# Decay attention and a mixer on one core: k of one pair turned by VectorE, the state's scan ahead of a masked copy, two loads a place later

## The chip, the cores and the metric

One core of a Trainium2 chip runs the whole computation in one launch. TensorE (PE) multiplies and transposes, VectorE (DVE) and ScalarE (ACT) work on its results in PSUM, GpSimd (POOL) works on data in SBUF, and SyncE (SP) issues nearly all loads and stores, which 16 DMA engines carry out. The metric is the device time of the launch in microseconds (us). A profile records one execution in which every instruction has a start and a duration. The page of the profile and the views quoted below are drawn from it.

## The reference

An attention with decay, in blocks of 64 rows, then a mixer over tokens and over channels. All arrays of the attention are float32; the mixer's four weights are float64.

```python
# q, k, v: (4, 8, 768, 64); lam: (8,)
for b in range(nb):                                    # blocks of 64 rows
    intra = einsum('bhic,bhjc->bhij', qb, kb) * Dmask  # lam ** (i - j), lower triangle
    intra = einsum('bhij,bhjd->bhid', intra, vb)
    inter = einsum('bhid,bhde->bhie', qb * lam_pow, kv_state)
    out[:, :, sl] = intra + inter
    kv_state = lam_block * kv_state + einsum('bhsd,bhse->bhde', kb * rev_pow, vb)
x = out.transpose(0, 2, 1, 3).reshape(4, 768, 512)

xt = x.transpose(0, 2, 1)
h = np.maximum(xt @ w_tok1, 0.0) @ w_tok2              # 768 -> 256 -> 768, over tokens
u = x + h.transpose(0, 2, 1)
h2 = np.maximum(u @ w_ch1, 0.0) @ w_ch2                # 512 -> 1536 -> 512, over channels
return u + h2
```

## The kernel before

**The attention stage.** The work is cut into 16 pairs of heads (4 batches, 4 pairs each), with rows in six blocks of 128. A loop written out by hand runs over `i` from -2 to 15; the instructions stand on each engine's queue in just this order, and each queue runs in order. Iteration `i` computes the scores of pair `i + 1`, the outputs of pair `i`, and prepares pair `i + 2`:

- `scores(i + 1)`, for each half `g` of the rows: PE multiplies k by q into two PSUM banks (`sc`, L304), and DVE multiplies them by the decay mask into SBUF (`a`, L312, "masked copy").
- `outputs(i, 0)`: PE adds scores times v (L328) and scaled q times state (L338); ACT copies the result to `uT` (L345).
- `state(i + 1)`: PE makes the products of k and v per block (`kv`, L270), DVE runs a scan over the blocks (`sv`, L278), and later, as `place()`, POOL copies it to `stb` (L291).
- `outputs(i, 1)`, the same for the second half.
- k and q of pair `i + 2` are turned so that the head dimension lies on partitions. For early pairs PE does it with transposes, three blocks to a PSUM bank, and ACT copies the bank out: `turn_q_rows` (L241, L242) for pairs below `NQ` = 5, `turn_k` (L220, L225) for pairs below `NKD` = 8. For later pairs DVE does it in one instruction (`turn_q` L230, `turn_kr` L234) from data that is loaded a second time, in another order, in pieces of 32 columns (`load_dims`, L115, four loads of 96 KB with rows of 128 bytes).
- `turn_back(i, g)`: PE turns the outputs back (`xp`, L360), ACT writes the high part `xhi` (L368), DVE the low part `xlo` (L369).
- `scale_k(i + 2)`: k times a decay, L250 on ACT and L252 on POOL; from pair `NKD` on both heads on ACT. `scale_q` (L257) is on POOL.

PSUM banks are taken in turn: three with the tag `sh`, and one `xT` that is lent out after the outputs. `kv`, `xp`, `kt`, `qt` and the groups of the mixer all share them, so that the next group on PE can wait for DVE's scan or for ACT's copy of an older one.

**The mixer's groups** fill the rest: from iteration 4 on, `take` says how many groups of the token mixer (`token_hidden` with `ph` L456, `hh` L460, `hl` L461; `token_out` with `pu` L493 and the addition L498) an iteration runs.

**The weights** come as float64 words and are made float32 by `narrow`: one step on ACT (L387) and four on DVE (L388, L391, L394, L397), then `split` into a high and a low part (L379 on ACT, L380 on POOL). These steps are put into a list `waiting`, and calls of `later(n)` between the other steps of the loop take a few off it. w1 comes in three parts, converted after iterations 0, 1 and 2; w2 comes in one load of 1536 KB, issued in iteration 3 and converted from iteration 5 on.

**The loads** of the loop all stand on SP's queue, in the order of the program. At the end of iteration `i`:

```python
if i == -1:
    load_w1(0)
if 0 <= i + 3 < NI and i >= -1:
    load_v(i + 3)
if i == -1:
    load_w1(1)
if i + 4 < NI:
    load_kq(i + 4)
if i == -1:
    load_w1(2)
if i == 3:
    load_w2()
```

`load_kq` issues k, q and, for pairs from `NKD` on, `kr`. The buffers of k, q and `kr` are two deep, those of v three.

After the loop the token mixer ends and the channel mixer runs to the end of the span; the change doesn't touch it.

Of the kernel before, what the change touches and what calls it, by code (L numbers as in the profile page):

```python
# [9 lines left out]
F32 = mybir.dt.float32  # L10
# [12 lines left out]
def kernel(  # L23
# [23 lines left out]
    nc = tc.nc  # L47
# [4 lines left out]
    P = 128  # L52
# [43 lines left out]
    ap = att.enter_context(tc.tile_pool(name="att", bufs=1))  # L96

    pairs = [(b, p) for b in range(B) for p in range(NP)]
# [3 lines left out]


    NQ = 5
    NKD = 8
    loaded = {}

    krs = {}
# [23 lines left out]
    def load_kq(i):  # L132
# [11 lines left out]
        else:  # L144
            load_dims(qn, q, b, p)
        if i >= NKD:
            kr = kp.tile([P, S], F32, tag="kr", bufs=2, name=f"kr{i}")
# [16 lines left out]
    mask = ap.tile([P, H, P], F32, name="mask")  # L164
# [35 lines left out]
    while n < P:  # L200
        nc.vector.tensor_mul(
            out=lamp[:, :, n : 2 * n], in0=lamp[:, :, 0:n], in1=lamp[:, :, n - 1 : n].broadcast_to([P, NP, n])
        )
        n *= 2
    for p in range(NP):
        nc.gpsimd.tensor_copy(
            out=keep[:, p, :, 1:], in_=lamp[:, p, P - 1 : P, None].broadcast_to([P, D, NC - 2])
# [4 lines left out]
    kTs, qTs, qss, kds, weights_of = {}, {}, {}, {}, {}  # L212
# [50 lines left out]
    def state(i):  # L263

        b, p = pairs[i]
        kv = bank("sh", f"kv{i}", D * (NC - 1))
        to = kv.rearrange("p (e c) -> p c e", c=NC - 1)
        for c in range(NC - 1):
            for h in range(2):
                nc.tensor.matmul(  # L270
                    out=to[h * D : (h + 1) * D, c, :],
                    lhsT=kds[i][:, h, c, :],
                    rhs=vns[i][:, h, c, :],
                    start=(c == 0),
                    stop=(c == NC - 2),
                )
        sv = ap.tile([P, D * (NC - 1)], F32, tag="sv", bufs=1, name=f"sv{i}")
        nc.vector.tensor_tensor_scan(  # L278
            out=sv,
            data0=keep[:, p].rearrange("p e c -> p (e c)"),  # L280
            data1=kv,
            initial=0.0,
            op0=ALU.mult,
            op1=ALU.add,
        )
        st = stb[i % 2]

        def place():
            for h in range(2):
                r = slice(h * D, (h + 1) * D)  # L290
                nc.gpsimd.tensor_copy(out=st[r, :, h, :], in_=sv[r].rearrange("p (e c) -> p c e", c=NC - 1))  # L291

        return place

    def scores(i):
        b, p = pairs[i]
        for g in range(2):
            pair = two_banks(f"sc{i}{g}", 3 * P)
            sc = [pair[:, h] for h in range(2)]
            for c in range(3):  # L300
                cs = slice((3 * g + c) * P, (3 * g + c + 1) * P)
                for h in range(2):
                    r = slice(h * D, (h + 1) * D)
                    nc.tensor.matmul(  # L304
                        out=sc[h][:, c * P : (c + 1) * P],
                        lhsT=kTs[i][r, cs],
                        rhs=qTs[i][r, cs],
                        start=True,
                        stop=True,
                    )  # L310
            a = ap.tile([P, 2, 3, P], F32, tag="a", bufs=4, name=f"a{i}{g}")
            nc.vector.tensor_mul(  # L312
                out=a,
                in0=pair.rearrange("p h (c i) -> p h c i", i=P),
                in1=mask[:, 2 * p : 2 * p + 2, None, :].broadcast_to([P, 2, 3, P]),
            )
            for h in range(2):
                weights_of[i, g, h] = a[:, h]

    def outputs(i, g):  # L320
        b, p = pairs[i]
# [80 lines left out]
    def words(b):  # L402
        return uT[b].rearrange("p t s -> p (t s)").bitcast(U32)

    def load_w1(i):
        cs = slice(2 * i, 2 * i + 2)
        nc.sync.dma_start(
            out=words(3).rearrange("p (c f) -> p c f", c=NC)[:, cs],
            in_=w_tok1.bitcast(U32).rearrange("(c s) f -> s c f", s=P)[:, cs],
        )  # L410
# [225 lines left out]
        groups.extend(hidden[b] + outs[b])  # L636
    take = {4: 2, 5: 2, 6: 2, 7: 5, 8: 4, 9: 4, 10: 5, 11: 2, 12: 2, 13: 4, 14: 3, 15: 1}
    early = {4: 2}
    LATE = 7
    idle = [lambda: None]  # L640
    held = [groups[n] for n in (36, 37, 33, 34, 35)]
# [5 lines left out]

    for i in range(-2, NI):
        if 0 <= i + 1 < NI:
            scores(i + 1)  # L650
            scale_q(i + 1)
        if i >= 0:
            outputs(i, 0)
        place = state(i + 1) if 0 <= i + 1 < NI else None
        work = [groups.popleft() for _ in range(take.get(i, 0))]
        if i == NI - 1:
            work.pop(0)()
        if i >= 0:
            outputs(i, 1)
            spare.append("xT")  # L660
        if i + 2 < NI and i != LATE:
            turn_q(i + 2)
            if i + 2 >= NKD:
                turn_kr(i + 2)
        if i + 2 < NI:
            if 0 < i + 2 < NP:
                masks(i + 2)
            turns = [(turn_k, 0), (turn_k, 1)] if i + 2 < NKD else []
            if i + 2 < NQ:
                turns += [(turn_q_rows, 0), (turn_q_rows, 1)]  # L670
            if i == -2:
                turns.sort(key=lambda x: x[1])
            for f, g in turns:
                f(i + 2, g)
        if place:
            place()
        later(0 if i == NI - 1 else 1 if work else 2)
        n = early.get(i, len(work) // 4)
        cuts = [0, n, max(n, (3 * len(work) + 1) // 4 if len(work) > 2 else len(work) // 2), len(work)]
        for n in range(3):  # L680
            for f in work[cuts[n] : cuts[n + 1]]:
                f()
                later(2 if len(work) < 3 else 1)
            if n < 2 and i >= 0:
                turn_back(i, n)
                later(1 if work else 2 + n)
            if n == 0 and i + 2 < NI:
                scale_k(i + 2)
        if i == -1:
            load_w1(0)  # L690
        if 0 <= i + 3 < NI and i >= -1:
            load_v(i + 3)
        if i == -1:
            load_w1(1)
        if i + 4 < NI:
            load_kq(i + 4)
        if i == -1:
            load_w1(2)
        if i == 3:
            load_w2()  # L700
        if 0 <= i < 3:
            convert_w1(i)
        if i == 5:
            weights[0] = group_tiles(0, False)
            w3 = words(3)
            load_piece(0, 0, w3[:, 2048:3072])
        if i == 4:
            convert_w2(0)
            convert_w2(1)
        if i == 5:  # L710
            convert_w2(2)
        if i == 6:
            waiting.append(lambda: load_piece(0, 1, w3[:, 1024:2048]))
            steps = narrow_piece(w3[:, 2048:3072], w3[:, 0:512], w3[:, 512:1024])
            turns = [lambda: turn_q(LATE + 2), lambda: turn_kr(LATE + 2)]
            waiting.extend(steps[:1] + 2 * idle + turns[:1] + idle + turns[1:] + idle + steps[1:2] + idle + steps[2:])
        if i == 7:
            steps = narrow_piece(w3[:, 1024:2048], w3[:, 512:1024], w3[:, 2048:2560])
            waiting.extend(steps[:1] + 2 * idle + steps[1:])
            waiting.append(lambda: load_piece(0, 2, w3[:, 2048:3072]))  # L720
        if i == 8:
            waiting.extend(split_c1(weights[0], w3[:, 0:512], w3[:, 512:1024], nc.gpsimd))
        if i == 9:
            waiting.append(lambda: load_piece(0, 3, w3[:, 1024:2048]))
            waiting.extend(narrow_piece(w3[:, 2048:3072], w3[:, 0:512], w3[:, 512:1024]))
            waiting.append(split_c2(weights[0], 2, w3[:, 0:512]))
        if i == 10:
            homes[0] = {"B11": (up, None, 1), "B21": (up, None, 1), "T2": (kp, "kn", 2), "T1": (kp, "qn", 2)}
            homes[0] |= {"B22": (kp, "kr", 2), "T3": (kp, "kT", 2), "T4": (kp, "qT", 2)}
            first = build(0, 0, on_vector=("T1", "T2", "T3", "T4", "B22"))  # L730
            waiting.extend([first["B11"], first["B21"]])
            waiting.extend(narrow_piece(w3[:, 1024:2048], w3[:, 2048:2560], w3[:, 2560:3072]))
            waiting.append(split_c2(weights[0], 3, w3[:, 2048:2560]))
        if i == 11:
            later(99)
        if i == 13:
            for xs in (("t1",), ("t2", "T1.h"), ("T2.h", "T1.l"), ("T2.l", "t3", "t4"), ("T3.h", "T4.h"), ("T3.l", "T4.l")):
                waiting.append(lambda xs=xs: [first[x]() for x in xs])
# [583 lines left out]
    for jj, x in [(jj, x) for jj in (1, 0) for x in range(4)]:  # L1322
        c, es, _, copy, queue = last_pieces[x]
# [30 lines left out]
```

## Time and profile before

| | |
|---|---|
| median of 3 runs | 554.91 us (554.79 to 555.17) |
| the profiled execution's own time | 554.8 us |
| its span, first to last instruction | 553.0 us |
| mean granted TensorE clock | 1.000 |
| busy: PE, DVE, ACT, POOL | 542.2, 437.2, 247.4, 281.6 us |
| attention stage | up to about 165 us |

The page gives busy time per engine; a busy PE isn't one at its peak, since ends of matmuls are modelled. The table of stages gives busy times for stretches of the span, the granted clock, the mean busy share of the 16 DMA engines and what they moved. In the lines of a timeline, the first two numbers are start and duration in us, and the bracket at the end, where there is one, is the time that the engine sat idle before it and who released it. The chain that ended last is followed back from the last instruction; its lines are start, duration, engine and line.

### The profile page before, as it was taken

The numbers are of one execution on the slowest core, as the hardware profiler recorded it, in microseconds if no ns is written. First come the engines' busy times: TensorE is split into PE (matmuls) and PEld (weight loads), VectorE is DVE, ScalarE is ACT, GpSimd is POOL, SyncE is SP. The second block draws the span as 40 slices with busy tenths as digits, with TensorE's granted clock in tenths as the row PEclk, the third lists the DMA queues.
The fourth block names the chain that finished last, engine by engine and source line by source line (L and its number), as shares of the span: only waits on it lengthen the run. The fifth ranks groups of instructions, "written<-read, shape, count | busy, mean of one in ns | idle before, by whom it ended". The sixth has DMA issues, their size and how long they took to land.

```text
span 553.0 us, 10803 instructions
## 1 busy us (share of the span) xinstructions
PE 542.2 (98%) x4180; PEld 528.3 (96%) x4180; DVE 437.2 (79%) x657; ACT 247.4 (45%) x499; POOL 281.6 (51%) x256
## 2 busy tenths in 40 slices
PE   6999999999999999999999999999999999999997
PEld 4888998999999999999999999999999999999996
DVE  4787889697786989887878878788777877788894
ACT  3464452335262554343444443443454555445431
POOL 5667453657214564444435444354475656568550
PEclk9999999999999999999999999999999999999999
DMA  9998999998203433361725300024767131220176
GB/s 182 252 208 170 232 186 176 195 196 145 50 2 98 181 114 124 101 223 39 248 78 181 142 1 1 0 30 59 149 137 199 58 116 57 86 105 2 22 155 129
DMA packets 175683, 66.77 MB, mean 121 GB/s; under 512 B 163600, under 2 KB 165904, under 8 KB 175632
## 3 DMA queue, kind: packets, MB, share of 16 engines
q1 hardware_dynamic: 170400, 64.90, 49.0%
q10 hardware_dynamic: 5232, 1.18, 1.0%
q8 instruction: 33, 0.54, 0.4%
q14 instruction: 18, 0.15, 0.1%
HBM read 49.29 MB, written 16.78 MB: 119 GB/s over the span
## 4 chain that ended last, share of the span: by engine, by line
PE 89%; DVE 4%; DMA 3%; ACT 1%; issue 1%; SPq 1%; ACTq 0%; DVEq 0%
PE po L1033 22%; PE pa L807 13%; PE pc L807 9%; PE pb L807 7%; PE pa L1007 7%; PE pc L1007 5%; PE ph L456 5%; PE sc L304 4%; PE pu L493 3%; PE xT L328 3%; PE pd L807 3%; DMA qn<-in_q_dram 3%; PE xT L338 2%; PE pu L476 2%; PE xp L360 1%; PE kv L270 1%
## 5 line engine op out<-in xcount | busy, mean ns | idle before, releaser
L1046 DVE TENSOR_TENSOR uT<-po,uT 128x768 f32<-128x768 f32 x57 | 54.2, 952 | 17.1 <-PE po L1033 16.8
L822 ACT ACTIVATE c<-c 128x384 f32<-128x384 f32 x42 | 22.1, 526 | 59.2 <-DVE c L867 33.5
L291 POOL COPY stb<-sv 64x320 f32<-64x320 f32 x32 | 26.7, 833 | 41.4 <-DVE sv L278 40.5
L1013 DVE TENSOR_TENSOR uT<-pa,uT 128x768 f32<-128x768 f32 x36 | 34.3, 953 | 10.3 <-PE pa L1007 9.6
L328 PE MATMUL xT<-a,vn 128*64 128x128 f32 x384 | 35.7, 277 | 0.0
L824 POOL TENSOR_TENSOR h22l<-c,h22h 128x384 fp32r<-128x384 f32 x14 | 14.4, 1032 | 41.5 <-ACT h22h L823 41.5
L345 ACT COPY uT<-xT 128x384 f32<-128x384 f32 x32 | 15.3, 479 | 44.2 <-PE xT L338 44.1
L1013 DVE TENSOR_TENSOR uT<-pc,uT 128x768 f32<-128x768 f32 x27 | 25.8, 954 | 11.2 <-PE pc L1007 11.2
L312 DVE TENSOR_TENSOR a<-sc,mask 128x768 f32<-128x768 f32 x32 | 29.1, 948 | 4.6 <-PE sc L304 4.5
L338 PE MATMUL xT<-qs,stb 128*64 128x128 f32 x320 | 31.3, 273 | 0.0
L380 POOL TENSOR_TENSOR c1l<-cs,c1h 128x512 fp32r<-128x512 f32 x15 | 19.3, 1298 | 23.1 <-ACT c1h L379 23.1
L456 PE MATMUL ph<-xhi,w1h 128*128 128x256 f32 x96 | 28.2, 293 | 0.7 <-DVE sv L278 0.4
L1033 PE MATMUL po<-h12h,c 128*128 128x384 f32 x112 | 28.7, 337 | 0.0
L1033 PE MATMUL po<-h11h,c 128*128 128x384 f32 x112 | 28.6, 336 | 0.0
L1033 PE MATMUL po<-h22h,c 128*128 128x384 f32 x112 | 28.6, 336 | 0.0
L1033 PE MATMUL po<-h21h,c 128*128 128x384 f32 x112 | 28.6, 336 | 0.0
L304 PE MATMUL sc<-qT,kT 64*128 64x128 f32 x384 | 27.1, 290 | 0.3 <-ACT qT L242 0.2
L304 PEld LDWEIGHTS sc<-qT,kT 64*128 64x128 f32 x384 | 23.9, 196 | 3.5 <-issue 1.7
L456 PE MATMUL ph<-xhi,w1l 128*128 128x256 f32 x96 | 27.1, 282 | 0.0
L456 PE MATMUL ph<-xlo,w1h 128*128 128x256 f32 x96 | 27.1, 282 | 0.0
L369 DVE TENSOR_TENSOR xlo<-xp,xhi 128x384 fp32r<-128x384 f32 x32 | 17.7, 553 | 11.0 <-ACT xhi L368 10.8
L257 POOL TENSOR_TENSOR qs<-qT,lamp 128x640 f32<-128x640 f32 x16 | 25.5, 1592 | 0.3
(397 smaller groups left out, 1944.0 us busy)
## 6 DMA issues: line engine op xcount, KB each, us to landing
raw<-in_moe_w_ch_dram SPq DMA_DIRECT2D x20, 512.0 KB, 3.7
vn<-in_v_dram SPq DMA_DIRECT2D x16, 384.0 KB, 5.3
kn<-in_k_dram SPq DMA_DIRECT2D x30, 192.0 KB, 5.4
out_dram<-y SPq DMA_DIRECT2D x104, 48.0 KB, 1.9
qn<-in_q_dram SPq DMA_DIRECT2D x44, 96.0 KB, 4.0
kr<-in_k_dram SPq DMA_DIRECT2D x32, 96.0 KB, 2.7
dc1h<-c1h SPq DMA_DIRECT2D x4, 768.0 KB, 5.3
dc1l<-c1l SPq DMA_DIRECT2D x4, 768.0 KB, 6.7
```

The lines of the kernel that those rows point to most:

```text
L257: nc.gpsimd.tensor_mul(out=qss[i], in0=qTs[i][:, P:].rearrange("p (c i) -> p c i", i=P), in1=lamp[:, p, None, :].broadcast_to([P, NC - 1, P]),
L291: nc.gpsimd.tensor_copy(out=st[r, :, h, :], in_=sv[r].rearrange("p (e c) -> p c e", c=NC - 1))
L304: nc.tensor.matmul(out=sc[h][:, c * P : (c + 1) * P], lhsT=kTs[i][r, cs], rhs=qTs[i][r, cs], start=True, stop=True,)
L312: nc.vector.tensor_mul(out=a, in0=pair.rearrange("p h (c i) -> p h c i", i=P), in1=mask[:, 2 * p : 2 * p + 2, None, :].broadcast_to([P, 2, ...
L328: nc.tensor.matmul(out=xT[h * D : (h + 1) * D, cs], lhsT=vns[i][:, h, c, :], rhs=weights_of[i, g, h][:, cg, :], start=(cg == 0), stop=False,)
L338: nc.tensor.matmul(out=xT[h * D : (h + 1) * D, cs], lhsT=st[:, c - 1, h, :], rhs=qss[i][:, c - 1, :], start=False, stop=(cg == 2),)
L456: nc.tensor.matmul(out=ph, lhsT=w[:, c, fs], rhs=x[:, c], start=(i == 0), stop=(i == 3 * NC - 1))
L807: nc.tensor.matmul(out=to, lhsT=w[:, t], rhs=x[:, t], start=(start and i == 0), stop=(i == 5), skip_group_check=not start,)
L1007: nc.tensor.matmul(out=pair[x][:, t], lhsT=w[:, t], rhs=h, start=(start and i == 0), stop=(i == 2), skip_group_check=not start,)
L1013: nc.vector.tensor_add(out=ub, in0=pair[x], in1=ub)
L1033: nc.tensor.matmul(out=to, lhsT=w[:, jj, t * P : (t + 1) * P], rhs=h, start=(i == 0), stop=(i == 3 * JG - 1))
L1046: nc.vector.tensor_add(out=ub, in0=po, in1=ub)
```

## The change

Three edits:

1. `NKD` goes from 8 to 7: k of the eighth pair (`i` = 7) is turned by DVE in `turn_kr(7)` in iteration 5 and not by PE in `turn_k(7, 0)` and `turn_k(7, 1)`. `load_kq(7)`, in iteration 3, loads `kr` of pair 7 as well, and `scale_k(7)` has both heads on ACT.
2. In pairs 3, 4, 5, 7 and 8 (`SCAN_FIRST`), the second masked copy (`g` = 1) is issued after `state`, and so behind the scan on DVE's queue.
3. Part 1 of w1 is loaded after k and q of pair 3, and part 2 after k and q of pair 4, an iteration later.

```diff
-    NKD = 8
+    NKD = 7
...
+    def mask_scores(i, g, pair):
+        p = pairs[i][1]
+        a = ap.tile([P, 2, 3, P], F32, tag="a", bufs=4, name=f"a{i}{g}")
+        nc.vector.tensor_mul(
+            out=a,
+            in0=pair.rearrange("p h (c i) -> p h c i", i=P),
+            in1=mask[:, 2 * p : 2 * p + 2, None, :].broadcast_to([P, 2, 3, P]),
+        )
+        for h in range(2):
+            weights_of[i, g, h] = a[:, h]
+
     def scores(i):
-        b, p = pairs[i]
         for g in range(2):
             pair = two_banks(f"sc{i}{g}", 3 * P)
...
-            a = ap.tile([P, 2, 3, P], F32, tag="a", bufs=4, name=f"a{i}{g}")
-            nc.vector.tensor_mul(
-                out=a,
-                in0=pair.rearrange("p h (c i) -> p h c i", i=P),
-                in1=mask[:, 2 * p : 2 * p + 2, None, :].broadcast_to([P, 2, 3, P]),
-            )
-            for h in range(2):
-                weights_of[i, g, h] = a[:, h]
+            if g == 0 or i not in SCAN_FIRST:
+                mask_scores(i, g, pair)
+        return pair
...
+    SCAN_FIRST = (3, 4, 5, 7, 8)
...
         if 0 <= i + 1 < NI:
-            scores(i + 1)
+            pair = scores(i + 1)
             scale_q(i + 1)
         if i >= 0:
             outputs(i, 0)
         place = state(i + 1) if 0 <= i + 1 < NI else None
+        if i + 1 in SCAN_FIRST:
+            mask_scores(i + 1, 1, pair)
...
         if 0 <= i + 3 < NI and i >= -1:
             load_v(i + 3)
-        if i == -1:
-            load_w1(1)
         if i + 4 < NI:
             load_kq(i + 4)
-        if i == -1:
-            load_w1(2)
+        if -1 <= i < 1:
+            load_w1(i + 2)
         if i == 3:
             load_w2()
```

## The prediction

> **What bounds the kernel now.** I read the page's first block, then the table of stages, then who waits for whom on TensorE (PE), and last the chain that ended last inside the attention stage.
>
> ```profile
> span 553.0 us, 10803 instructions
> PE 542.2 (98%) x4180; PEld 528.3 (96%) x4180; DVE 437.2 (79%) x657; ACT 247.4 (45%) x499; POOL 281.6 (51%) x256
> ...
> core 0: us, PE busy (x) PEld busy (x) DVE busy (x) ACT busy (x) POOL busy (x), PEclk, DMA share, GB/s
> 54.00:57.00 3.00, 3.00 (x66) 2.88 (x64) 2.66 (x4) 1.09 (x3) 0.00 (x0) 1.00 0.96 369
> 64.00:66.50 2.50, 2.50 (x43) 2.38 (x44) 2.38 (x4) 0.94 (x3) 2.50 (x2) 1.00 1.01 161
> ...
> 20.00:58.00 38.00, 37.22 (x545) 33.44 (x543) 30.35 (x44) 20.44 (x47) 24.29 (x23) 1.00 1.00 216
> 58.00:95.00 37.00, 36.57 (x421) 33.53 (x418) 31.68 (x52) 16.78 (x36) 17.87 (x16) 1.00 1.00 185
> 95.00:178.00 83.00, 82.90 (x935) 78.85 (x935) 64.69 (x98) 34.34 (x69) 37.77 (x32) 1.00 0.59 114
> ```
>
> PE is busy 98% of the span at a granted clock of 1.00, so at first sight only PE work counts. But everything the diff touches runs before 95 us, and there the DMA engines are full too: share 1.00 in 20:58 and again in 58:95, against 0.59 after 95. DVE works 31.7 of the 37 us in 58:95. The chain shows which of the three sets the pace:
>
> ```profile
> 58.05 0.24 PE xT L338 x4
> 58.32 0.48 ACT uT L345
> 58.80 0.69 ACT kT L225 x2
> 59.53 0.69 ACT uT L387
> 60.63 0.56 DVE xlo L369
> ...
> 70.97 0.86 DVE kT L234
> ...
> 78.06 0.87 DVE a L312
> ...
> 84.38 1.32 PE pu L493 x6
> ...
> 94.29 0.48 DVE uT L498
> 94.81 1.22 PE ph L456 x8
> ```
>
> From 58.3 to 84.4 the chain does not touch PE at all. It goes through ScalarE and VectorE, from the first step of w2's conversion (L387 at 59.53) to the additions at L498, and PE takes it up only at 84.38 and 94.81. PE looks busy throughout, but it has no slack: it runs at the chain's pace. What starts the chain at 59.5 is the important question, because both first steps of that conversion read w2:
>
> ```profile
> 51.83 0.53 SPq L422 DMA_DIRECT2D uT<-in_moe_w_tok_dram  x1
> 52.45 0.41 SPq L157 DMA_DIRECT2D vn<-in_v_dram  x1
> ...
> uT<-in_moe_w_tok_dram SPq DMA_DIRECT2D x1, 1536.0 KB, 7.3
> ...
> 59.10 0.72 DVE L388 TENSOR_SCALAR uT<-uT 128x512 uint32<-128x512 uint32 x1 [0.35 <-DMA uT<-in_moe_w_tok_dram]
> ```
>
> w2 is issued at 51.83 and lands 7.3 us later, at 59.1, and DVE already sits idle 0.35 us for it. ScalarE's own first step on w2 starts at 59.53, held by the two kT copies ahead of it. So w2 has 0.43 us to spare (59.53 - 59.10) and no more.
>
> **The change part by part.**
>
> *k of pair 7 by VectorE: what goes.* Six transposes on PE, the two kT copies on ScalarE, and one POOL multiply of scale_k, which becomes a second ScalarE multiply.
>
> ```profile
> 58.20 0.88 PE L220 MATMUL kt<-ident,kn 128*128 128x128 f32 x6
> 58.91 0.49 PE L360 MATMUL xp<-ident,uT 128*128 128x128 f32 x3
> ...
> 57.80 0.95 DVE L230 STREAM_TRANSPOSE qT<-qn 128x768 f32<-128x768 f32 x1
> ...
> 60.47 0.57 ACT L250 ACTIVATE kd<-kn,mask 128x320 f32<-128x320 f32 x1
> 73.54 1.00 ACT L250 ACTIVATE kd<-kn,mask 128x320 f32<-128x320 f32 x2
> ```
>
> PE gets back 58.91 - 58.20 = 0.71 us. ScalarE loses the copies (0.7 us in the chain) and gains 1.00 - 0.57 = 0.43 us of kd behind xhi; hh of the next group, which stands behind it, is not in the chain, so I cost that at nothing; uncovered it costs its 0.43.
>
> *What comes: one DVE transpose, some 0.9 us, as for kT of pair 8 (0.86 in the chain).* It stands right behind qT of pair 7, which starts at 57.80 and takes 0.95, and so runs at about 58.7 to 59.6. If DVE is waiting for w2 there, it is free; if not, it costs its full 0.9 us. And it needs four loads of 96 KB more, kr of pair 7, which load_kq(7) issues in iteration 3. Iteration 3 is where load_w2 stands directly behind, on the same SP queue.
>
> ```profile
> 63.31 2.23 SPq L115 DMA_DIRECT2D kr<-in_k_dram  x4
> 65.65 0.47 SPq L157 DMA_DIRECT2D vn<-in_v_dram  x1
> ```
>
> The four kr loads of pair 8 hold SP from 63.31 to the next issue at 65.65: 2.34 us. That is the term that decides. w2 is issued today straight behind the last qn load (48.18 + 3.60 = 51.78, row below), so nothing there takes the shift up: w2 goes out at 51.83 + 2.34 = 54.17 and lands at 54.17 + 7.3 = 61.47. Bounds: by bytes alone, 4 x 96 KB = 393 KB at the 369 GB/s of 54:57 (w2 alone) is 1.07 us; at the 161 GB/s of 64:66.5 (kr of pair 8 alone) 2.44 us. I take 2.34, since it is the same instruction at the same place one iteration on. SP blocked behind a fuller queue can add about 1 us more: qn takes 3.60 us for four issues where kr takes 2.23.
>
> ```profile
> 48.18 3.60 SPq L115 DMA_DIRECT2D qn<-in_q_dram  x4
> ```
>
> The Trainium skill, "DMA: Bandwidth & Descriptors", section "Issuing engines are not separate DMA queues", calls the sequencer's time to start a DMA usually small beside the DMA itself; by that the price would be the transfer's alone, and at w2's rate the run would end like rival (a) below. The rows disagree for pieces as small as these: four issues fill 2.34 us, about as long as their bytes at the 161 GB/s measured for them. The same page's "Specifications" speaks against (a), too: it asks for 512 B or more for the full rate, and kr comes in rows of 128 B; 161 against 369 GB/s agrees.
>
> What stands behind the wait: ScalarE's L387 for w2 is ahead of xhi of pair 5, kd of pair 7 and hh in its queue; DVE's L388 is ahead of xlo, hl and the masked copies of pair 7. PE waits for those through the shared PSUM banks. ScalarE's start moves from 59.53 to 61.47, **+1.94 us**. From there to 94.81 the chain is ScalarE and DVE work that does not shrink, so PE takes the delay over where the chain reaches it, at 84.38 and 94.81 at the latest.
>
> *Scan ahead of the second masked copy, pairs 3, 4, 5, 7, 8.* DVE work is the same; sv is ready earlier by one masked copy, about 0.9 us (0.87 in the chain, L312), and the second copy later by one scan. The second copy is read a whole iteration later (some 10 us), so its delay costs nothing. sv releases the PSUM bank that the next group on PE takes. What PE loses there now:
>
> ```profile
> 26.84 0.84 PE L241 MATMUL qt<-ident,qn 128*128 128x128 f32 x6 [0.25 <-DMA qn<-in_q_dram]
> 47.06 0.87 PE L220 MATMUL kt<-ident,kn 128*128 128x128 f32 x6
> 48.37 0.39 PE L456 MATMUL ph<-xhi,w1h 128*128 128x256 f32 x1 [0.43 <-DVE sv L278]
> ...
> 81.12 0.56 DVE L369 TENSOR_TENSOR xlo<-xp,xhi 128x384 fp32r<-128x384 f32 x1 [0.15 <-ACT xhi L368]
> ```
>
> The 0.43 us at 48.37 (pair 5) should go. Next in line there would be the transposes of k ahead on PE, which end at about 47.9. At pair 8 the earlier sv lets PE and then ScalarE hand on xhi sooner, and DVE's 0.15 us at 81.12 may go: I take **-0.2 us**, as that lies inside the chain; ends 0 and -0.5. The scan could now hold DVE until PE's kv is done. In these pairs it starts today straight behind the second copy, so kv is done by then; at worst DVE idles one copy, 0.87 us, per pair. I take nothing, as DVE runs behind PE here, being what the chain waits for. The bound lies within the 1 us of rival (c).
>
> *w1's parts a place later.* k and q of pair 3 go ahead of part 1, and v, k and q of pair 4 ahead of part 2; the bytes up to w2 stay the same. The 0.25 us at 26.84 goes.
>
> ```profile
> 15.89 2.77 SPq L407 DMA_DIRECT2D uT<-in_moe_w_tok_dram  x1
> 18.82 2.22 SPq L137 DMA_DIRECT2D kn<-in_k_dram  x2
> 21.15 2.50 SPq L140 DMA_DIRECT2D qn<-in_q_dram  x2
> 23.70 0.78 SPq L407 DMA_DIRECT2D uT<-in_moe_w_tok_dram  x1
> ...
> 33.75 0.96 DVE L388 TENSOR_SCALAR uT<-uT 128x512 uint32<-128x512 uint32 x1
> 41.64 0.69 ACT L387 ACTIVATE uT<-uT 128x512 f32<-128x512 f32 x1
> ```
>
> Part 1 goes out some 5 us later (2.22 + 2.50), near 21, and even with w2's 7.3 us to land it is there at 28, ahead of its first reader at 33.75. Part 2, before at 23.70, is moved past the same and one v load more, some 6 us, and by the same reckoning is there by 37, ahead of 41.64. Cost nothing; if that cover went, DVE would stand still as at w2.
>
> **The sum.** PE's own savings ahead of 59 us are 0.71 + 0.25 + 0.43 = 1.4 us, but they end in front of the wait for w2: the chain behind w2 is started by the DMA queue, not by PE. What counts is +1.94 - 0.2 = +1.7 us. After 95 us PE runs without a gap (82.90 of 83 us), so nothing there gives it back. The profiled execution took 554.8 us (span 553.0), 0.1 under the median of 554.91: 554.8 + 1.7 = **556.5 us**, 0.3% slower. Its own range: w2 later by 1.75 to 3.4 us gives 555.9 to 557.5.
>
> **The rivals.** (a) *No measurable change*: kr's bytes fill gaps that the DMA queue has before w2, and w2 is only about 1.07 us late. ScalarE then starts at 60.17, +0.64, less 0.2: 555.2. For it speaks that the new order of w1 may free SP earlier (the 2.77 us block at 15.89); against it, that the total of bytes ahead of w2 grows and SP issues without a pause there. It decides from a delay under 1.75 us. (b) *Faster*: w2 lands no later than PE can use it, so PE keeps its 1.4 us and the 0.2: 553.2. That takes a DMA queue that makes up the 2.34 us and about 1.0 more (1.4 less the 0.43 in hand) by 51 us, by the new order of w1 alone; one block of 2.77 us is all I see that could be saved. (c) *Slower still*: the whole queue is 2.3 us behind, and loads of pairs 8 to 10 come late for DVE's transposes too, say another 1 us: 557.5. Against it, DVE itself is late by nearly as much.
>
> **How the numbers follow.** A measurement of this kernel can tell about 0.2%, 1.1 us, from no change. The forecast 0.55, (c) 0.08, (a) 0.22, (b) 0.15. The first two are slower except for a small share: slower 0.62, same 0.23, faster 0.15. Of 2 in 10 left out, most is (b), so the range goes from 553.5 to 557.9.
>
> **What would show it.** Right: L422 issued near 54, and DVE's L388 for w2 idle about 2 us or more with w2 as releaser, at about 61.4; PE waiting in 64 to 80 for xlo, h or kT, and in all 1 to 3 us more idle in 58:95. No wait for sv near 48, none for qn near 27, kt x6 gone near 58. Wrong: w2 landing before 60.2 (rival a), or PE's work behind 95 us starting earlier than before.

## The result and the profile after

| | median us (lowest to highest, runs) | profiled execution | span |
|---|---|---|---|
| before | 554.93 (554.63 to 555.17, 6) | 554.8 | 553.0 |
| changed | 558.79 (557.47 to 560.71, 6) | 559.21 | 557.3 |

The ratio is 1.007 (95%: 1.0057 to 1.0083): slower, as forecast, but by 3.9 us where +1.7 was forecast, and above the range. In three later sessions the same kernel took 557.2, 556.87 and 557.49 us, +2.1 to +2.9 on the kernel before in the same session. Both sizes are explained below as far as the runs allow. Two single executions, 664.4 us of `after_look3` (the profiled one, so that run has no profile to read) and 1077.13 us of `no_kr`, lie far outside all others and are left out of the medians and ratios below.

The first block of the page of the changed kernel, and then its table of stages:

```profile
span 557.3 us, 10795 instructions
PE 541.5 (97%) x4174; PEld 527.6 (95%) x4174; DVE 438.0 (79%) x658; ACT 247.3 (44%) x498; POOL 280.3 (50%) x255
```

```profile
core 0: us, PE busy (x) PEld busy (x) DVE busy (x) ACT busy (x) POOL busy (x), PEclk, DMA share, GB/s
20.00:58.00 38.00, 37.57 (x552) 34.35 (x551) 31.73 (x45) 20.62 (x47) 25.17 (x23) 1.00 0.95 197
58.00:95.00 37.00, 31.93 (x384) 29.06 (x383) 28.12 (x46) 13.40 (x29) 13.43 (x13) 1.00 0.99 201
95.00:178.00 83.00, 82.65 (x934) 78.02 (x933) 64.37 (x99) 36.81 (x73) 38.62 (x34) 1.00 0.63 120
```

PE has six instructions fewer and the clock is 1.00 as before. The time is lost in one stage: in 58:95 PE is busy 31.93 us where it was 36.57, 4.6 us less. In 20:58 it is even 0.35 us busier, and after 95 it runs almost without a gap (82.65 of 83 us). The load queue (SP) of the changed kernel shows what comes in ahead of that stage; columns are start, duration, engine, line, operation:

```profile
47.86 4.18 SPq L115 DMA_DIRECT2D qn<-in_q_dram  x4
52.09 2.34 SPq L115 DMA_DIRECT2D kr<-in_k_dram  x4
54.48 0.63 SPq L427 DMA_DIRECT2D uT<-in_moe_w_tok_dram  x1
...
56.20 6.87 SPq L137 DMA_DIRECT2D kn<-in_k_dram  x2
```

The new kr loads of pair 7 take 52.09 to 54.48, and w2 (L427; L422 before) goes out 2.65 us later than before. ScalarE and DVE, in their timelines, stand still for it:

```profile
63.17 0.69 ACT L392 ACTIVATE uT<-uT 128x512 f32<-128x512 f32 x1 [5.53 <-DMA uT<-in_moe_w_tok_dram]
...
64.12 1.01 ACT L250 ACTIVATE kd<-kn,mask 128x320 f32<-128x320 f32 x2
65.04 0.37 ACT L465 ACTIVATE hh<-ph 128x256 fp32r<-128x256 f32 x1
```

```profile
57.52 0.94 DVE L234 STREAM_TRANSPOSE kT<-kr 128x768 f32<-128x768 f32 x1
63.17 0.43 DVE L393 TENSOR_SCALAR uT<-uT 128x512 uint32<-128x512 uint32 x1 [4.72 <-DMA uT<-in_moe_w_tok_dram]
```

The first step on w2 starts at 63.17 on ScalarE (59.53 before) and on DVE (59.10 before). The bracket is the idle time ahead of an instruction and what ended it: 5.53 us on ScalarE, 4.72 on DVE, both for w2. The new kT of pair 7 (0.94 us at 57.52) ends at 58.46, where that wait of DVE begins: it only fills time in which DVE would have stood for w2 anyway. PE takes the delay over through its waits (total, times, longest) in 58:95, first of the changed kernel, then of the one before:

```profile
PE xT L333 <- DVE xlo L374: 3.6, 3, 1.4
PE xp L365 <- DVE sv L278: 0.5, 1, 0.5
PE kv L270 <- DVE h L466: 0.5, 1, 0.5
PE pu L498 <- DVE uT L503: 0.4, 1, 0.4
```

```profile
PE ph L456 <- DVE uT L498: 0.2, 1, 0.2
```

The chain of the changed kernel between 50 and 100 us is now mostly loads:

```profile
54.48 8.68 DMA uT<-in_moe_w_tok_dram
63.17 0.44 DVE uT L393
...
67.06 2.74 DMA kr<-in_k_dram
...
89.40 4.18 DMA uT<-in_moe_w_ch_dram
```

w2 is one link, but kr of pair 8 and the channel weights (w_ch), which stand behind w2 on the same queue, are links too.

### The profile page after: what moved, and what is told of

Its sections match the earlier page's. It is cut to its first block, busy times and chain, and to the rows that moved or that the text cites. A ratio compares the mean times of both kernels' runs of the same rounds, so it can differ in the third digit from the quotient of the medians.

```text
span 557.3 us, 10795 instructions
## 1 busy us (share of the span) xinstructions
PE 541.5 (97%) x4174; PEld 527.6 (95%) x4174; DVE 438.0 (79%) x658; ACT 247.3 (44%) x498; POOL 280.3 (50%) x255
## 4 chain that ended last, share of the span: by engine, by line
PE 82%; DVE 6%; DMA 4%; SPq 3%; issue 1%; ACT 1%; ACTq 1%; POOL 1%; DVEq 0%
PE po L1039 21%; PE pa L813 12%; PE pc L813 9%; PE pb L813 7%; PE pa L1013 7%; PE pc L1013 5%; PE ph L461 4%; PE pu L498 3%; PE pd L813 3%; PE sc L314 3%; SPq L115 3%; PE xT L333 2%; PE xT L343 2%; DMA uT<-in_moe_w_tok_dram 2%; PE pu L481 1%
## 5 line engine op out<-in xcount | busy, mean ns | idle before, releaser
L333 PEld LDWEIGHTS xT<-a,vn 128*64 128x64 f32 x384 | 22.3, 137 | 6.1 <-DVE xlo L374 4.0
```

The source lines that it names most:

```text
L333: nc.tensor.matmul(out=xT[h * D : (h + 1) * D, cs], lhsT=vns[i][:, h, c, :], rhs=weights_of[i, g, h][:, cg, :], start=(cg == 0), stop=False,)
```

## The experiments

All ratios are against the kernel before, run on the same chip in the same session. Its medians there were 554.58 to 554.80.

**Which part costs: kr alone, all but kr, kr's loads alone, all but kr's loads.** `only_kr` is the kernel before with one line changed:

```diff
-    NKD = 8
+    NKD = 7
```

> The kernel before with the first edit alone (k of pair 7 by VectorE, its four kr loads ahead of w2). Theory 'w2 is late': w2 goes out about 2.3 to 2.7 us later and lands at 61.5 to 63.2, ScalarE's L387 starts with it, and the run ends at 557 to 560 us, as the changed kernel. Rival 'the order of scan and copies, or of w1, is to blame': 553.5 to 555.5, since neither is in it.

`no_kr` is the changed kernel with that line taken back (scan order and w1's place remain).

> The changed kernel with k of pair 7 still turned by TensorE (NKD = 8): the scan order and w1's new place alone. Theory 'w2 is late': w2 lands near 59.1 as before; TensorE's waits at 27 and 48 us go, but the chain behind w2 starts at most 0.4 us earlier, so 554.2 to 555.0 us. Rival 'the order of scan and copies, or of w1, is to blame': 556.5 us or more. Rival 'TensorE bounds': 0.25 + 0.43 us saved and more, 554.0 or less.

`loads_only` is the kernel before, which also loads kr of pair 7 and doesn't use it:

```diff
-        if i >= NKD:
+        if i >= NKD - 1:   # in load_kq: kr of pair 7 too
```

> The kernel before, which also issues the four kr loads of pair 7 at their place ahead of w2 but doesn't use them: TensorE still turns k of pair 7. Theory 'w2 is late': 557.5 to 559.5 us, w2 landing at 61.5 to 63.2. Rival 'the work on VectorE and ScalarE (kT and kd of pair 7) costs the time': 554.9 us, as before.

`no_loads` is the changed kernel without these four loads; DVE turns q of pair 7 in place of k, so the scores of that pair are other ones, with the same engine work:

```diff
-        if i >= NKD:
+        if i == NKD:
+            krs[i] = qn
+        elif i > NKD:
```

> The changed kernel without the four kr loads of pair 7: VectorE turns the array of q a second time in place of k, so that kT of pair 7 holds q's values and the scores of that pair are other ones; all engine work is as in the changed kernel. Theory 'w2 is late': w2 lands near 59.1, ScalarE's L387 starts at 59.1 instead of 59.53, and the run ends at 554.0 to 554.7 us. Rival 'the work on VectorE and ScalarE costs the time': 557 us or more.

| | median us | ratio (95%) |
|---|---|---|
| only_kr | 556.57 | 1.0034 (1.0021 to 1.0047) |
| no_kr | 553.72 | 0.9988 (0.9980 to 0.9997) |
| loads_only | 556.91 | 1.0046 (1.0031 to 1.0060) |
| no_loads | 554.06 | 0.9994 (0.9986 to 1.0002) |

The loads alone, with no work moved between engines, cost 2.3 us (556.91 against 554.61). All the engine work of the change without the loads costs nothing that can be measured. Without kr the other two parts are a gain of 0.9 us. The sizes missed what was expected: only_kr and loads_only ended below their ranges (from 557 and 557.5 us), and no_kr fell below the 554.2 to 555.0 of the theory into what "TensorE bounds" allowed (554.0 or less). ScalarE's timelines at the first step on w2, in this order loads_only, no_loads, no_kr:

```profile
60.67 0.68 ACT L387 ACTIVATE uT<-uT 128x512 f32<-128x512 f32 x1 [1.12 <-DMA uT<-in_moe_w_tok_dram]
...
62.08 0.37 ACT L460 ACTIVATE hh<-ph 128x256 fp32r<-128x256 f32 x1
64.21 0.62 ACT L379 CAST w2h<-uT 128x512 fp32r<-128x512 f32 x1 [1.76 <-DVE uT L397]
```

```profile
59.95 0.69 ACT L394 ACTIVATE uT<-uT 128x512 f32<-128x512 f32 x1 [2.26 <-DMA uT<-in_moe_w_tok_dram]
```

```profile
58.27 0.68 ACT L392 ACTIVATE uT<-uT 128x512 f32<-128x512 f32 x1
```

The profiled execution of no_loads was the slowest of its twelve (555.92 us, median 554.06). Its queue was late without any new load: w2 went out at 53.26, 1.43 us later than in the kernel before. So the queue's own place moves from run to run, and these start times are to be read beside their own spans.

In no_kr ScalarE has no bracket, and its step comes 1.26 us earlier (59.53 to 58.27); the span is 1.2 shorter. Both things that hold this stage back came earlier: PE's transposes of k, whose copies ScalarE makes first (58.20 to 56.94), and w2 itself, for which DVE waits as briefly as before (0.43 us, 0.35 before):

```profile
57.93 0.65 DVE L393 TENSOR_SCALAR uT<-uT 128x512 uint32<-128x512 uint32 x1 [0.43 <-DMA uT<-in_moe_w_tok_dram]
```

Whether the scan order or w1's place brought the gain is not known: no run has one of them without kr.

**The changed kernel again, and kr with one of the other two parts.** `after_again`, `after_look3` and `after_look4` are the changed kernel unaltered. `kr_scan` is the changed kernel with w1's loads at their old place; `kr_w1` is the changed kernel with the old order of scan and masked copy.

> The changed kernel once more, beside the next three on one chip. Theory 'w2 is late': the span follows w2's landing one for one, as in the six profiles so far (before: landing 59.08, span 553.0; loads_only 60.65 and 554.4; only_kr 60.82 and 554.8; changed kernel 63.15 and 557.3). So whatever its median is, between 557.5 and 560.7 us, span less landing comes out at 493.5 to 494.2.

> The kr edit with the scan order, w1 at its old place. The changed kernel is some 2 us above only_kr. If w1's new place brings that (the DMA queue comes to w2 later, w1 part 1 having taken 3.1 us to land there instead of 1.5), this one ends at 556.0 to 557.0 us, as only_kr. If the scan order brings it, 558 us or more.

> The kr edit with w1 at its new place, the scan order as before. If w1's new place brings the other 2 us of the changed kernel: 558 to 559.5 us, with a wider spread, and w2 issued at 54 or later. If the scan order brings them: 556 to 557 us.

> The changed kernel a third time (558.79 and 557.2 us so far). Theory 'w2 is late': span less ScalarE's start on w2 is 494.0 within 0.2, as in its other two profiles (494.13 and 493.92), and its time lies between 556.5 and 559.5 us with the place of w2's landing. If the difference of the two earlier medians came from elsewhere, this remainder moves and not the landing.

> The changed kernel as it is, for a profile beside the next two. Theory 'w2 is late': span less ScalarE's start on w2 is 494.0 within 0.2, wherever between 60.5 and 63.5 us w2 lands.

| | median us | ratio (95%) |
|---|---|---|
| after_again | 557.20 | 1.0044 (1.0031 to 1.0057) |
| after_look3 | 556.87 | 1.0049 (1.0033 to 1.0064) |
| after_look4 | 557.49 | 1.0047 (1.0031 to 1.0063) |
| kr_scan | 556.22 | 1.0026 (1.0016 to 1.0036) |
| kr_w1 | 556.92 | 1.0040 (1.0026 to 1.0055) |

The three repeats agree with each other, and not with the 1.007 of the first session: the 2 us between the changed kernel and only_kr, which kr_scan and kr_w1 were to divide, did not come again. (w1's part 1, for which the expectation of kr_scan gives 3.1 and 1.5 us, took 6.3 us from issue to landing in the changed kernel and 7.6 in only_kr.) ScalarE's timeline of after_again:

```profile
60.98 0.68 ACT L392 ACTIVATE uT<-uT 128x512 f32<-128x512 f32 x1 [2.47 <-DMA uT<-in_moe_w_tok_dram]
...
62.85 0.37 ACT L465 ACTIVATE hh<-ph 128x256 fp32r<-128x256 f32 x1
64.53 0.62 ACT L384 CAST w2h<-uT 128x512 fp32r<-128x512 f32 x1 [1.31 <-DVE uT L402]
```

w2 is used 2.2 us earlier than in the first session, and the span is 2.4 shorter (554.9). Put beside each other, the profiles in which w2 comes in one load on SP's queue give one rule:

| kernel | first step on w2 | span | span less that start |
|---|---|---|---|
| no_kr | 58.27 | 551.8 | 493.53 |
| nkd9 (below) | 59.18 | 553.0 | 493.82 |
| before | 59.53 | 553.0 | 493.47 |
| no_loads | 59.95 | 554.0 | 494.05 |
| kr_w1 | 60.40 | 554.5 | 494.10 |
| after_look4 | 60.40 | 554.4 | 494.00 |
| kr_scan | 60.49 | 554.5 | 494.01 |
| loads_only | 60.67 | 554.4 | 493.73 |
| only_kr | 60.84 | 554.8 | 493.96 |
| after_again | 60.98 | 554.9 | 493.92 |
| changed, first session | 63.17 | 557.3 | 494.13 |
| kd_pool (below) | 64.07 | 557.8 | 493.73 |

Over 5.8 us of starts the rest of the run stays between 493.47 and 494.13 us. The start on w2 is thus a good mark of what was lost until then, whatever held it: in the kernel before and in no_kr that was the copies of kT, in the others w2. Scan order and w1's place can't be told from nothing once kr is in (the intervals of only_kr, kr_scan and kr_w1 overlap); that kr_w1 is 0.7 above kr_scan stays open.

**The 0.4 us of the second kd multiply.** `kd_pool` is the changed kernel with pair 7's second scale_k multiply back on POOL:

```diff
-            if h == 0 or i >= NKD:
+            if h == 0 or i >= NKD + 1:
```

> The changed kernel with the second decay multiply of pair 7 on POOL, as in the kernel before. If that multiply on ScalarE is the 0.5 us by which span less ScalarE's start on w2 is larger (494.0 against 493.5): 493.4 to 493.7 here, and about 0.5 us off the time. If it is hidden: 494.0 and no change.

It measured 556.68 us, 1.0037 (1.0023 to 1.0052), beside after_look4's 557.49: 0.8 less, but the intervals overlap. Its profiled execution was the slowest of its six (559.65 us). Its ScalarE, and then the kernel before's:

```profile
64.07 0.68 ACT L392 ACTIVATE uT<-uT 128x512 f32<-128x512 f32 x1 [4.27 <-DMA uT<-in_moe_w_tok_dram]
...
65.46 0.39 ACT L465 ACTIVATE hh<-ph 128x256 fp32r<-128x256 f32 x1
```

```profile
61.59 0.39 ACT L460 ACTIVATE hh<-ph 128x256 fp32r<-128x256 f32 x1 [0.54 <-PE ph L456]
```

hh comes 1.39 us after the first step on w2 here (65.46 - 64.07), 1.41 in loads_only, but 1.87 in the changed kernel, in both sessions (65.04 - 63.17, 62.85 - 60.98). w2h doesn't care: 3.55 us in after_again, 3.54 in loads_only. In the table the five kernels with one kd on ScalarE leave 493.47 to 493.82 (mean 493.66), the seven with two 493.92 to 494.13 (mean 494.02). So about 0.4 us of it may reach the end. That it does so by way of hh isn't shown: in the kernel before hh comes 2.06 us after the start on w2 (61.59 - 59.53, held by PE), later than in any of these, and its rest is the shortest of all (493.47). Nor does the timing show the 0.4 us for certain.

**w2 in pieces.** If only the wait for w2 counts, then w2 loaded in four pieces, cut where the three conversions are cut, should end it. `after_thirds` is the changed kernel with

```diff
-        nc.sync.dma_start(
-            out=words(2).rearrange("p (k s) -> p k s", k=NK),
-            in_=w_tok2.bitcast(U32).rearrange("(k f) s -> f k s", f=P),
-        )
+        to = words(2).rearrange("p (k s) -> p k s", k=NK)
+        src = w_tok2.bitcast(U32).rearrange("(k f) s -> f k s", f=P)
+        n = 2 * S
+        for kk, a, z in ((0, 0, 2 * n // 3), (0, 2 * n // 3, n), (1, 0, n // 3), (1, n // 3, n)):
+            nc.sync.dma_start(out=to[:, kk, a:z], in_=src[:, kk, a:z])
```

`nokr_thirds` is the same with `NKD = 8`. `nkd9` and `nkd9_thirds` have `NKD = 9`, so that kr of pair 8 is gone too, with w2 whole and in pieces.

> The changed kernel with w2 loaded in four pieces at the same place, cut along the three conversions, so that the first conversion waits for a third of w2 alone. Theory 'w2 is late': the first third lands some 3.5 us ahead of the whole, near 59.5, so the chain starts as early as in the kernel before or earlier: 553.3 to 555.5 us, 3 us or more under the changed kernel. Rival 'the work on VectorE and ScalarE, or the later kr loads, cost the time': no change, 557.5 us or more.

> The changed kernel with NKD = 8 and w2 in four pieces. Revised theory 'the whole load queue is the limit up to 95 us': the first third lands about 1.7 us earlier than the whole did (57.9), and kr of pair 8 and the first piece of w_ch come at their old times, so part of the gain is lost to those: 552.3 to 553.3 us. Theory 'only the wait for w2 counts': 552.0 us or less.

> The changed kernel with k of pair 8 turned by TensorE, too (NKD = 9): four kr loads fewer than in the kernel before, behind w2 on the queue; 0.7 us more on TensorE, 0.9 us less on VectorE inside its chain. If w2's landing alone counts: as no_kr, 553.4 to 554.0 us. If VectorE's chain behind it counts as well: 552.8 to 553.3 us. If TensorE is the limit: 554.3 us or more.

> NKD = 9, the scan order, w1's new place, and w2 in four pieces: a shorter wait for w2 and 2.3 us less on the load queue behind it. Revised theory 'the whole load queue is the limit up to 95 us': 551.5 to 552.8 us, below nokr_thirds. If the loads behind w2 don't matter: as nokr_thirds within 0.3 us.

| | median us | ratio (95%) |
|---|---|---|
| after_thirds | 556.64 | 1.0036 (1.0022 to 1.0050) |
| nokr_thirds | 554.81 | 1.0003 (0.9991 to 1.0015) |
| nkd9 | 554.11 | 0.9992 (0.9984 to 1.0001) |
| nkd9_thirds | 553.81 | 0.9987 (0.9978 to 0.9996) |

All four came out above what the theory under test gave them, nkd9 by 0.1 us only (554.0 was the most if w2's landing alone counts), and this is the most telling miss. In after_thirds the wait for w2 is gone, yet the time isn't. Its ScalarE, then its DVE:

```profile
57.59 0.68 ACT L392 ACTIVATE uT<-uT 128x512 f32<-128x512 f32 x1
...
80.87 0.68 ACT L392 ACTIVATE uT<-uT 128x512 f32<-128x512 f32 x1 [2.37 <-DMA uT<-in_moe_w_ch_dram]
```

```profile
70.12 0.98 DVE L234 STREAM_TRANSPOSE kT<-kr 128x768 f32<-128x768 f32 x1 [1.05 <-DMA kr<-in_k_dram]
```

The first step on w2 starts 1.94 us earlier than before the change (59.53 to 57.59). But DVE then waits 1.05 us for kr of pair 8, and ScalarE 2.37 us for the first channel weights (w_ch), the longer of two waits for them (3.9 us in all). SP's timelines show how late the queue is when w_ch goes out: the kernel before, loads_only and after_thirds.

```profile
74.25 0.53 SPq L530 DMA_DIRECT2D uT<-in_moe_w_ch_dram  x1
```

```profile
75.66 0.53 SPq L530 DMA_DIRECT2D uT<-in_moe_w_ch_dram  x1
```

```profile
53.43 2.23 SPq L431 DMA_DIRECT2D uT<-in_moe_w_tok_dram  x4
...
76.50 0.53 SPq L536 DMA_DIRECT2D uT<-in_moe_w_ch_dram  x1
```

In loads_only, w_ch goes out 1.4 us later than before. The pieces have a price of their own: four issues take 2.23 us where one takes 0.53, and in after_thirds w_ch is another 0.8 later. That they cost even without kr is seen in ScalarE's wait in nokr_thirds; and that the queue is late with w2 whole, too, in after_again, whose rows (total, times, longest, 50 to 100 us) stand second:

```profile
ACT uT L392 <- DMA uT<-in_moe_w_ch_dram: 1.7, 1, 1.7
```

```profile
ACT uT L392 <- DMA uT<-in_moe_w_tok_dram: 2.5, 1, 2.5
...
ACT uT L392 <- DMA uT<-in_moe_w_ch_dram: 1.0, 1, 1.0
```

Neither before nor no_kr has such a wait for w_ch. Nor do loads_only, only_kr and after_look4, though their w_ch goes out 1.0 to 1.7 us later than before, as in after_again (1.6): whether the wait appears is a close thing, since the engines, having waited for w2, are late as well. So it isn't one late load: the queue behind w2 has next to no slack either, and where the wait for w2 is taken away, the one for w_ch appears. How after_thirds' 1.8 us divide between kr and the pieces is not settled. In nkd9_thirds, with fewer loads and w2 in pieces, ScalarE and DVE wait for no load in that stretch, and the time is that of no_kr, 0.9 us below the kernel before, with six more transposes on PE. What else could be had without the loads isn't shown.

**w2 from another queue.** `w2_act` is the changed kernel with `nc.scalar.dma_start` in place of `nc.sync.dma_start` for w2, so that no issue on SP stands ahead of it.

> The changed kernel with w2 issued from ScalarE's queue, at the same place of the program, so that it no longer stands behind the kr loads in SP's queue. If SP's issue time is the price: w2 lands before 59 us and the time is 554 to 555.3 us. If the bytes are (all queues share the 16 DMA engines): w2 lands earlier but q and kr of pair 7 land 3 us or more later, VectorE waits for them at 57 instead, and the time is 556 us or more.

It took 558.33 us, 1.0068 (1.0053 to 1.0083). ScalarE, SP and DVE of w2_act:

```profile
46.35 0.38 ACTq L427 DMA_DIRECT2D uT<-in_moe_w_tok_dram  x1
...
61.12 0.68 ACT L392 ACTIVATE uT<-uT 128x512 f32<-128x512 f32 x1
```

```profile
48.41 8.25 SPq L115 DMA_DIRECT2D qn<-in_q_dram  x4
56.71 2.24 SPq L115 DMA_DIRECT2D kr<-in_k_dram  x4
```

```profile
42.77 0.98 DVE L230 STREAM_TRANSPOSE qT<-qn 128x768 f32<-128x768 f32 x1 [2.37 <-DMA qn<-in_q_dram]
```

w2 goes out 8.1 us earlier and nothing waits for it any more. But the four qn issues beside it now take 8.25 us where they took 4.18. Here the rule of the table ends: span less start is 495.28 us (556.4 - 61.12), and ScalarE waits 1.2 us for w_ch. The time is in the range that was expected if the bytes are the price (556 us or more). It can't be put down to the edit, since in this execution DVE had already lost 2.37 us for q of pair 5 at 42.77, ahead of w2's issue. So the run fits with loads that share the engines whoever issues them, and leaves open what w2's own place is worth.

The best versions are no_kr and nkd9_thirds, each 0.9 us below the kernel before in its session. The first is the plain one: leave `NKD` at 8 and keep the other two parts.

## Why the prediction missed the size

**The chain and its start: right.** With w2 in one load, what bounds the stage is when w2 is there, and what makes it late is the kr loads on SP's queue. loads_only shows that these loads cost the time with no other edit, and the table of starts shows the span following one for one.

**The issue of w2: right.** 54.17 was forecast, 54.48 came. The parts: qn began 0.32 earlier (47.86 against 48.18) and took 0.58 longer, and kr held SP for 2.39 us where 2.34 was set down. The forecast took 48.18 as given, and that the parts nearly cancel is in part luck: in loads_only, whose program up to there is that of the kernel before, qn began at 47.06.

**The landing of w2: the step that failed.** "Lands at 54.17 + 7.3 = 61.47" took the flight as fixed. In after_again and after_look4 it held (7.3 and 7.2 us; the first step on w2 at 60.98 and 60.40, even earlier than forecast, as qn began earlier). In the profiled execution of the first session it took 8.7 us, and ScalarE's start moved by 3.64 instead of 1.94 us; w2 landed 4.1 us later than before, where the range went to 3.4. This is most of the miss. The span ended 2.56 us above the forecast (557.3 against 553.0 + 1.74): 1.70 are this start (63.17 against 61.47), 0.66 a longer rest of the run (494.13 against 493.47), and 0.2 the gain of the scan order, which was taken off and isn't seen. The other five executions of that session have no profile. The transfers during w2's flight, for the kernel before, the changed kernel in the first session, and after_again:

```profile
DMA packets 2423, 2.00 MB, mean 276 GB/s; under 512 B 2167, under 2 KB 2167, under 8 KB 2423
...
uT<-in_moe_w_tok_dram SPq DMA_DIRECT2D x1, 1536.0 KB, 7.3
```

```profile
DMA packets 4381, 2.39 MB, mean 276 GB/s; under 512 B 4123, under 2 KB 4123, under 8 KB 4379
...
uT<-in_moe_w_tok_dram SPq DMA_DIRECT2D x1, 1536.0 KB, 8.7
```

```profile
DMA packets 3482, 2.16 MB, mean 297 GB/s; under 512 B 3225, under 2 KB 3225, under 8 KB 3481
...
uT<-in_moe_w_tok_dram SPq DMA_DIRECT2D x1, 1536.0 KB, 7.3
```

w2 flies among small packets from loads around it: 2167 before, 4123 in the long flight. That these made it longer is likely, not shown, since a longer flight also meets more packets. In after_again 0.16 MB more than before flew beside w2 and it was as quick, at 297 GB/s. Nor is it the state of the engines at the issue alone: in the first half microsecond their share is 0.15 before, but 1.00 in the long flight and 1.06 in after_again. So a fixed flight doesn't price a load here, and why it was 8.7 us that once stays open.

**kd of pair 7 on ScalarE, costed at nothing: probably a second miss,** of about 0.4 us, by the means of the table; by which way it would reach the end is open, as said there. The two profiled repeats add up so: the first step on w2 later by 1.45 and 0.87 us, the rest longer by 0.45 and 0.53, spans 554.9 and 554.4, +1.9 and +1.4. They were the fastest of their sessions' runs (556.77 and 556.15 us); the medians lie 0.4 and 1.3 higher, and where w2 landed in those runs isn't recorded.

**PE's savings of 1.4 us, worth nothing: right with kr's loads, not without.** The waits for sv at 48.37 and for qn at 26.84 are gone, as forecast, and the transposes of pair 7 with them; new ones came for qT at 41.63 (0.43 us) and, behind the wait for w2, for sv at 73.06 (0.54). In no_kr, where PE and w2 are both there earlier, the scan order and w1's place bring 0.9 us.

**Scan order, -0.2; w1's place, nothing:** too small to see beside kr.

**The rivals.** (a) and (b) are out: the queue did not make up the loads. (c), the whole queue late, was given 0.08, with "DVE itself is late by nearly as much" against it. That tells who waits first, and the waits for w_ch (1.0 us in after_again) show that the queue is late behind w2 too. The first session ended beyond (c)'s 557.5; in its profiled execution most of that came through w2's landing, not through those later loads.

**The rule on issuing: set aside wrongly.** The Trainium skill, "DMA: Bandwidth & Descriptors", section "Issuing engines are not separate DMA queues", says that loads started by any engine end on the same 16 DMA engines, and that issuing from several saves the sequencer's time alone. The prediction held that the rows disagree. They don't need to: 393 KB in 2.39 us is 164 GB/s, near the 161 measured for such rows (in 64:66.5, which holds the last rows of q, of the same 128 B, beside those of kr), so SP's time can be the transfers' own, backed up into the queue (argued, not shown). w2_act agrees with the rule as far as it goes: w2 flies from ScalarE's queue, and SP's qn issues grow from 4.18 to 8.25 us.

**Its own signs.** "DVE idle about 2 us or more for w2": 4.72, with w2 as releaser, but at 63.17 and not at about 61.4. "1 to 3 us more idle in 58:95" on PE: 4.6, of which xlo alone ended 3.6.

## What to carry to other kernels

In a stage where the DMA share is 1.00, price an added load by the time its bytes take at the rate of its row size (here 2.44 us at 161 GB/s, and 1.4 to 2.9 were measured outside the first session), and charge it to the whole queue behind it: where the one wait that shows is removed, the next reader may be found to have no slack either. Work taken off the busiest engine was worth nothing measurable here beside the loads that it needed; the two parts that add no load were a gain by themselves. A difference of a few us in one session, with a kernel whose time hangs on one load's landing, should be seen again in a second session before its size is explained.

## What was not expected of the hardware

The queue stood behind a large load. SP's next kn issues stood until w2 had about landed: in the kernel before from 54.32 to 59.07 (w2 there at 59.1), in the changed kernel from 56.20 to 63.07 (w2 there at 63.16). And one 1536 KB load, issued behind the same instructions, took 7.2 to 8.7 us to land in three executions of one kernel, and the changed kernel's whole time ran from 556.08 to 560.71 us over its four sessions, where the kernel before kept to 554.16 to 555.81.
